# A routed mixture of experts behind attention: when a small block's weights are requested, and the order of the first two blocks

## The chip, the cores and the metric

The kernel runs on one core of a Trainium2 chip. The metric is the device time of one execution in microseconds, the median of the runs shown. TensorE does matrix products, VectorE and ScalarE elementwise work and the eviction of products, GpSimd the indirect DMAs (gather and scatter of rows by an index), SyncE issues the other DMAs.

## The reference

Three stages follow one another; each token is a row of 384 numbers.

```python
def reference(...):
    attn_out = _attn_ref(q, k, v, a_re, a_im)       # 4 x 8 heads, 768 steps, 48 wide: a recurrent state
    x = attn_out.transpose(0, 2, 1, 3).reshape(3072, 384)
    x = np.maximum(np.maximum(x @ w1, x @ w2), x @ w3) @ w_out    # first, dense layer
    ...
    # second layer, 8 experts: each row goes to the one expert with the largest logit
    logits = normed(x) @ normed(expert_emb).T / tau
    expert_idx = np.argmax(logits, axis=1)
    for e in range(8):
        mask = expert_idx == e
        h = np.maximum(x[mask] @ w1[e], 0.0)        # w1[e]: 384 x 1024
        out[mask] = gate_w[mask, None] * (h @ w2[e])  # w2[e]: 1024 x 384
```

## The kernel before, in words

The first part (to about 592 us of the trace) computes attention and the dense layer and writes its 3072 rows to memory. A first routing, over the rows that were done early, has by then chosen the rows of the first blocks. The second part, `phase2` (L1325), is the layer of experts, and the change lies there.

**Blocks and steps.** Rows of one expert are gathered into blocks of 128. `STEPS` (L56) lists what is done in order: steps 0 and 1 are single blocks (blocks 0 and 1, of the same expert), steps 2 to 6 and 8 to 13 are pairs of blocks that share an expert's weights (256 rows), and step 7 is one single block. In a pair, each product is made of three with operands split into a high and a low part (fp32r); single blocks use fp32 for the first product. An expert with only a few rows left (at most 32) is a **small block**, done by `small` (L1271), a generator in pieces that are placed into the steps that `WITH` (L58) names: 4, 6, 8, 10 and 12.

**What a step issues.** The loop of `phase2` goes through the steps; in step k it calls `gather` (L1173) for the rows of step k+2 on GpSimd, `load(k + 1)` (L1159) for the expert's weights, and `prep` (L1181), which copies and splits these weights into the form the products use (ScalarE copies to `w1s` and `w2h`, L1197 and L1206; VectorE subtracts to `w1l` and `w2l`, L1207). Then come the two halves of the first product, `mm1` (L1230: eviction to `hhi` on ScalarE, L1249, and to `hlo` on VectorE, L1250), `transpose` of the next step's gathered rows (L1217), and the second product `mm2` (L1254), which ends in a scatter of the rows to `out` on GpSimd. A small block of step k+1 begins in step k: its expert number is read on SyncE, both its weights are requested (`w1m`, L1281, and `w2m`, L1282), and its rows are gathered. Its products stand between the step's.

**What sets the order.** The program is written in the order above, and a scheduler moves instructions within each engine; afterwards each engine and each DMA queue works strictly in its own order. All weight DMAs go through SyncE. The regular weights have a ring of two slots (`QD = 2`): `load(k)` waits for a slot whose last reader (a copy or a subtraction in `prep`) is done. A load is conditional (`cond=c`): in this run's data six of the loads name the expert before and are skipped. `w1m` and `w2m` have one buffer each (`bufs=1`), so the DMA of the next small block waits until the small block before has made its first product (for `w1m`) or its second (for `w2m`). While SyncE waits there, everything behind it waits.

**The opening.** Steps 0 and 1 are run together (L1380 to L1383): step 0's products, then step 1's rows transposed, then step 1's first product. In these steps and the next two, `late_route` (L1066) runs on VectorE: the routing of the remaining rows, in two pieces (`LATE = 1, 1`, both placed behind step 1), whose end gives the list `src` from which the blocks of step 4 and later are gathered. The routing's tables lie in a pool (`rtp`) that is closed then, and the small blocks' weights (`mp`) take its place.

Of the kernel before, what the change touches and what calls it, by code (L numbers as in the profile page):

```python
# [9 lines left out]
F32 = mybir.dt.float32  # L10
# [15 lines left out]
DM = H * D  # L26
# [19 lines left out]
def steps(order):  # L46

    out, p, s = [(0, 1), (1, 1)], 2, KP
    for c in order:
        out.append((p, 2) if c == "p" else (s, 1))  # L50
        p, s = (p + 2, s) if c == "p" else (p, s + 1)
    assert (p, s) == (KP, NBLK - SPARE)
    return out + [(i, 1) for i in range(s, NBLK)]


STEPS = steps("ppppp" "s" "pppppp")  # L56

WITH = 4, 6, 8, 10, 12  # L58
NE, NS = 1 + PE, len(STEPS)

TESTS = 6 * NU + 6 + NTILE
# [252 lines left out]
class Prog:  # L314
# [956 lines left out]
    def small(self, pool, mp, pg, m):  # L1271


        nc = self.nc
        t, v, s, g = nc.tensor, nc.vector, nc.scalar, nc.gpsimd
        i, KD, KF, Q = NBLK + m, DM // 128, FF2 // 128, FF2 // 4
        e = nc.values_load(self.mtab[0:1, m:m + 1], engines=[ET.SP], min_val=0, max_val=E - 1,
                           skip_runtime_bounds_check_because="a count of 8 comparisons, of which one fails")
        w1 = mp.tile([128, KD, FF2], F32, tag="w1m", bufs=1, name=f"w1m{m}")
        w2 = mp.tile([128, KF, DM], F32, tag="w2m", bufs=1, name=f"w2m{m}")  # L1280
        nc.sync.dma_start(w1, self.io["w21"][bass.ds(e, 1)].rearrange("a p (k f) -> p (a k) f", f=FF2))  # L1281
        nc.sync.dma_start(w2, self.io["w22"][bass.ds(e, 1)].rearrange("a p (k f) -> p (a k) f", f=DM))  # L1282
        xg = pool.tile([128, DM], F32, tag="xg", bufs=4, name=f"xgm{m}")
        g.indirect_dma_start(out=xg, out_offset=None, in_=self.x1d,
                             in_offset=bass.IndirectOffsetOnAxis(ap=self.src[:, i:i + 1], axis=0),
                             bounds_check=NT - 1, oob_is_err=False)
        yield
        px = pg.tile([128, KD, MT], F32, tag="px", bufs=2, name=f"pxm{m}")
        for k in range(KD):
            t.transpose(px[:, k], xg[:MT, k * 128:(k + 1) * 128], self.ident[:MT, :MT])  # L1290
        x = pool.tile([128, KD, MT], F32, tag="xT", bufs=2, name=f"xm{m}")
        s.copy(x, px)
        yield
        ph = pg.tile([128, Q], F32, tag="ph", bufs=3, name=f"phm{m}")
        for k in range(KD):
            for j in range(4):
                t.matmul(ph[j * MT:(j + 1) * MT], x[:, k], w1[:, k, j * Q:(j + 1) * Q], start=k == 0, stop=k == KD - 1,
                         skip_group_check=True)
        h = mp.tile([128, Q], F32, tag="hm", bufs=1, name=f"hm{m}")
        s.activation(h, ph, AF.Relu)  # L1300
        yield
        pt = pg.tile([128, 2, 128], F32, tag="px", bufs=2, name=f"pt{m}")
        for c in range(2):
            t.transpose(pt[:, c], h[:, c * 128:(c + 1) * 128], self.ident)
        hT = mp.tile([128, 2, 128], F32, tag="hT", bufs=1, name=f"hT{m}")
        v.tensor_copy(hT, pt)
        yield
        py = pg.tile([128, DM], F32, tag="py", bufs=2, name=f"pym{m}")
        for c in range(2):
            for j in range(4):  # L1310
                r = slice(j * MT, (j + 1) * MT)
                t.matmul(py[r], hT[:, c, r], w2[:, 2 * j + c], start=c == 0, stop=c == 1, skip_group_check=True)
        part = pool.tile([128, DM], F32, tag="yo", bufs=3, name=f"part{m}")
        s.copy(part, py)
        yield
        ps = pg.tile([128, DM], F32, tag="py", bufs=2, name=f"psm{m}")
        t.matmul(ps, self.four, part, start=True, stop=True)
        y = pool.tile([128, DM], F32, tag="yo", bufs=3, name=f"ym{m}")
        s.activation(y, ps, AF.Copy, scale=self.gate_of[:, i:i + 1])
        g.indirect_dma_start(out=self.io["out"], in_=y, in_offset=None,  # L1320
                             out_offset=bass.IndirectOffsetOnAxis(ap=self.dst[:, i - KE:i - KE + 1], axis=0),
                             bounds_check=NT - 1, oob_is_err=False)
        yield

    def phase2(self):  # L1325
        tc, nc = self.tc, self.nc
        with ExitStack() as ctx:
            regs = tc.queue_regs(depth=QD, engines=[ET.SP, ET.Activation, ET.DVE], name="wr")

            pool = ctx.enter_context(tc.tile_pool(name="m2", bufs=1, reuse_waits="tile"))  # L1330
            qp = ctx.enter_context(tc.tile_pool(name="wq", bufs=1, reuse_waits="tile"))
            q1 = qp.queue([128, 3072], F32, regs=regs, name="q1", contiguous=True)
            q2 = qp.queue([128, 3072], F32, regs=regs, name="q2", contiguous=True)
            pg = ctx.enter_context(tc.tile_pool(name="pg2", bufs=2, space=PSUM, reuse_waits="tile"))
            wq = ctx.enter_context(tc.tile_pool(name="ws", bufs=1, reuse_waits="tile"))

            late_ctx = ctx.enter_context(ExitStack())
            rp = late_ctx.enter_context(tc.tile_pool(name="rtp", bufs=1, reuse_waits="tile"))
            load, gather, prep, share, transpose, mm1, mm2, st = self.moe2(pool, wq, pg, regs, q1, q2)
            late = self.late_route(rp, pg)  # L1340
            gather(*STEPS[1])
            load(0)
            first = prep(*STEPS[0])
            for _ in range(2):
                next(first)
            last = NS - SPARE
            few = iter(())
            for k, (i, n) in enumerate(STEPS[:last]):
                if k + 2 < last:
                    gather(*STEPS[k + 2])  # L1350
                p, after = iter(()), k + 1 < last
                if k == 0:

                    share(*STEPS[:2])
                    p = first
                elif after:
                    load(k + 1)
                    p = prep(*STEPS[k + 1])
                if k + 1 in WITH:

                    small = self.small(pool, mp, pg, WITH.index(k + 1))
                    next(small)
                next(p, 0)
                if k != 1:
                    mm1(i, n, 0)

                for _ in few:
                    pass
                if k in WITH:
                    few = small_now  # L1370
                    next(few)
                if k + 1 in WITH:
                    small_now = small
                next(p, 0)
                if k != 1:
                    mm1(i, n, 1)
                next(few, 0)
                next(p, 0)
                if after:
                    transpose(*STEPS[k + 1])  # L1380
                if k == 0:

                    for h in range(2):  # L1383
                        mm1(*STEPS[1], h)
                for b in range(n):
                    next(p, 0)
                    mm2(i, n, b)
                    next(few, 0)
                for _ in p:
                    pass  # L1390
                for _ in range(LATE.count(k)):
                    next(late)
                if k == LATE[-1]:
                    late_ctx.close()

                    self.four = self.mask
                    nc.gpsimd.memset(self.four, 0.0)
                    nc.vector.tensor_reduce(self.four[:, :MT], self.ident.rearrange("p (j r) -> p r j", r=MT), axis=AX.X,
                                            op=ALU.add)
                    mp = ctx.enter_context(tc.tile_pool(name="mp", bufs=1, reuse_waits="tile"))  # L1400
# [289 lines left out]
```

## Time and profile before

| | |
|---|---|
| median of 3 runs | 877.92 us (877.83 to 882.82) |
| the profiled execution | 880.89 us |
| its span, from the first instruction to the last | 879.1 us |
| mean granted TensorE clock, share of full speed | 0.972 |
| second part, first to last product | 592.35 to 871.79 |

All rows come from the one profiled execution; its 880.89 holds the span and 1.8 us around it. In a timeline row the first number is the start in us from the span's start, the second the duration; then engine, line of the kernel, operation, out<-in (the programs' names, buffer numbers left out), shape and count; in brackets the idle time of the engine ahead of it and what ended that. A row may stand for several instructions, back to back (x3). A row of the windows view begins with the window's start and end, each cut at the first product of a step (the six shown are steps 3, 5, 8, 9, 10 and 11), and gives its length, the busy time of each engine with its instructions, the mean granted clock of TensorE, and the DMA engines' share and rate.

### The profile page before, as it was taken

The page shows a single profiled execution, that of the slowest core. Times are in us where ns is not written, and L with a number is a line of the kernel's source. Part 1 is how long each engine was busy: PE and PEld are TensorE (multiplying, and loading weights), DVE is VectorE, ACT ScalarE, POOL GpSimd, SP SyncE. Part 2 cuts the span into 40 slices and gives each one's busy share as a digit, 9 for nine tenths or more (in the row PEclk, how much of TensorE's full clock was granted, in tenths as well). Part 3 has the DMA queues.
Part 4 walks back from the last instruction along what each step waited for, and adds up shares of the span by engine and source line. Part 5 has one row for each costly group of instructions (what it writes and reads, how often), then busy time and mean ns, then how long its engine had stood idle before and what let it go on. Part 6 is the DMA issues. An engine that isn't in the chain of part 4 may idle for free. (4 is left out here: it accounts for less than half of the span.)

```text
span 879.1 us, 17501 instructions
## 1 busy us (share of the span) xinstructions
PE 814.8 (93%) x6741; PEld 716.4 (81%) x6741; DVE 643.7 (73%) x1371; ACT 434.3 (49%) x918; POOL 132.7 (15%) x195
## 2 busy tenths in 40 slices
PE   0877899999999999999999999998968989999996
PEld 0655697979897888889797978888968989889986
DVE  5998898899888899898898854447984553545531
ACT  7897636435554536564546241117334563645521
POOL 5541100010100000000001000021123313222201
PEclk9889899999999999999999999998997999999999
DMA  8641162433625170707162341050036757475200
GB/s 316 250 115 30 35 138 82 109 122 69 160 45 147 32 187 18 175 17 174 43 149 83 72 88 32 19 191 26 29 152 223 303 215 285 164 298 216 96 20 23
DMA packets 38989, 108.67 MB, mean 124 GB/s; under 512 B 5460, under 2 KB 27011, under 8 KB 35824
## 3 DMA queue, kind: packets, MB, share of 16 engines
q1 hardware_dynamic: 30032, 77.15, 30.6%
q0 software_dynamic: 8320, 29.52, 10.1%
q8 instruction: 55, 0.90, 0.5%
q10 hardware_dynamic: 544, 0.79, 0.3%
q14 instruction: 38, 0.31, 0.1%
HBM read 97.92 MB, written 10.62 MB: 123 GB/s over the span
## 5 line engine op out<-in xcount | busy, mean ns | idle before, releaser
L299 PE MATMUL ph<-xhi,whi 128*128 128x256 f32 x648 | 117.1, 289 | 0.4 <-DVE slotgate L299 0.4
L299 PE MATMUL ph<-xlo,whi 128*128 128x256 f32 x648 | 112.8, 283 | 0.0
L299 PE MATMUL ph<-xhi,wlo 128*128 128x256 f32 x648 | 112.8, 283 | 0.0
L299 PEld LDWEIGHTS ph<-xhi,whi 128*128 128x128 f32 x648 | 93.5, 191 | 2.7 <-PE slots L299 0.5
L299 PEld LDWEIGHTS ph<-xlo,whi 128*128 128x128 f32 x648 | 93.2, 192 | 0.0
L299 PEld LDWEIGHTS ph<-xhi,wlo 128*128 128x128 f32 x648 | 93.1, 191 | 0.0
L1245 PE MATMUL ph<-xh,w1s 128*128 128x256 f32 x264 | 77.0, 292 | 1.2 <-DVE hlo L1250 1.2
L1261 PE MATMUL py<-w2h,hhi 128*128 128x384 f32 x200 | 71.2, 356 | 5.6 <-ACT hhi L1249 5.6
L1207 DVE TENSOR_TENSOR w2l<-queue_q_buf,w2h 128x768 fp32r<-128x768 f32 x52 | 47.9, 954 | 38.2 <-ACT w2h L1206 38.0
L1245 PE MATMUL ph<-xh,w1l 128*128 128x256 f32 x264 | 74.6, 283 | 0.0
L1245 PE MATMUL ph<-xl,w1s 128*128 128x256 f32 x264 | 74.6, 283 | 0.0
L1261 PE MATMUL py<-w2h,hlo 128*128 128x384 f32 x200 | 70.7, 355 | 3.5 <-DVE hlo L1250 3.3
L1250 DVE SCALAR_TENSOR_TENSOR hlo<-ph,hhi 128x512 fp32r<-128x512 f32 x50 | 34.3, 687 | 50.6 <-ACT hhi L1249 50.6
L299 PE MATMUL px<-wo,h 128*128 128x392 f32 x192 | 71.2, 502 | 0.0
L1261 PE MATMUL py<-w2l,hhi 128*128 128x384 f32 x200 | 69.7, 348 | 0.0
L299 DVE TENSOR_TENSOR h<-ph,h 128x512 f32<-128x512 f32 x72 | 49.5, 688 | 25.7 <-PE ph L299 23.6
L299 PEld LDWEIGHTS pa<-S 112*128 112x128 f32 x384 | 50.1, 196 | 8.9 <-ACT kt L299 4.7
L299 PE MATMUL pa<-S 112*128 112x128 f32 x384 | 53.2, 282 | 4.2 <-ACT kt L299 4.2
L299 PE MATMUL py<-at,v 128*64 128x128 f32 (+1 forms) x576 | 56.4, 276 | 0.4 <-DVE at L299 0.4
L1249 ACT ACTIVATE hhi<-ph 128x512 fp32r<-128x512 f32 x50 | 29.6, 597 | 50.9 <-PE ph L1245 50.7
L1245 PEld LDWEIGHTS ph<-xh,w1s 128*128 128x128 f32 x264 | 50.4, 191 | 4.6 <-issue 2.5
L299 PE MATMUL py<-S,Ts 112*64 112x128 f32 x480 | 51.5, 291 | 0.0
(405 smaller groups left out, 1846.4 us busy)
## 6 DMA issues: line engine op xcount, KB each, us to landing
queue_q_buf<-w SPq DMA_DIRECT2D x26, 1536.0 KB
S<-QK SPq DMA_DIRECT2D x46, 289.1 KB
QKr<-qk SPq DMA_DIRECT2D x11, 768.0 KB
X<-a SPq DMA_DIRECT2D x10, 768.0 KB
w1m<-w SPq DMA_DIRECT2D x5, 1536.0 KB
w2m<-w SPq DMA_DIRECT2D x5, 1536.0 KB
v<-v POOLq DMA_DIRECT2D x24, 288.0 KB
x1d<-x1s SPq DMA_DIRECT2D x20, 192.0 KB
```

Source lines behind the costliest of these rows:

```text
L299: getattr(getattr(self.nc, c[0]), c[1])(*c[2], **c[3])
L1207: v.tensor_sub(lo, bv[:, c], hi.bitcast(F32))
L1245: t.matmul(ph[:, f], a, b, start=o == 0, stop=o == len(ops) - 1)
L1249: s.activation(hi, ph, AF.Relu).ins,
L1250: v.scalar_tensor_tensor(lo, ph, 0.0, hi.bitcast(F32), op0=ALU.max, op1=ALU.subtract).ins]
L1261: t.matmul(py, a[:, f, r], c[:, k % 4], start=o == 0, stop=o == 3 * KF - 1)
```

## The change

Three edits. (1) In `small` the tile and the DMA of the second weights `w2m` move behind a new `yield`, so they are requested by a second call of the generator; `phase2` makes that call at the start of the step in which the small block is computed, behind `load(k + 1)`. The gather of the small block's rows stays in the first call. (2) `WITH` names the steps 5, 7, 9, 11 and 12 in place of 4, 6, 8, 10 and 12, so the first call of the first small block comes in step 4's place of the loop and the last one's products stay in step 12. (3) In step 0 the transposition of step 1's rows comes ahead of step 0's first product.

```diff
-WITH = 4, 6, 8, 10, 12
+WITH = 5, 7, 9, 11, 12
...
         w1 = mp.tile([128, KD, FF2], F32, tag="w1m", bufs=1, name=f"w1m{m}")
-        w2 = mp.tile([128, KF, DM], F32, tag="w2m", bufs=1, name=f"w2m{m}")
         nc.sync.dma_start(w1, self.io["w21"][bass.ds(e, 1)].rearrange("a p (k f) -> p (a k) f", f=FF2))
-        nc.sync.dma_start(w2, self.io["w22"][bass.ds(e, 1)].rearrange("a p (k f) -> p (a k) f", f=DM))
         xg = pool.tile([128, DM], F32, tag="xg", bufs=4, name=f"xgm{m}")
         g.indirect_dma_start(out=xg, out_offset=None, in_=self.x1d,
                              in_offset=bass.IndirectOffsetOnAxis(ap=self.src[:, i:i + 1], axis=0),
                              bounds_check=NT - 1, oob_is_err=False)
+        yield
+
+        w2 = mp.tile([128, KF, DM], F32, tag="w2m", bufs=1, name=f"w2m{m}")
+        nc.sync.dma_start(w2, self.io["w22"][bass.ds(e, 1)].rearrange("a p (k f) -> p (a k) f", f=DM))
         yield
...
                     load(k + 1)
                     p = prep(*STEPS[k + 1])
+                if k in WITH:
+                    next(small_now)
                 if k + 1 in WITH:
 
                     small = self.small(pool, mp, pg, WITH.index(k + 1))
                     next(small)
                 next(p, 0)
+                if k == 0:
+                    transpose(*STEPS[1])
                 if k != 1:
                     mm1(i, n, 0)
...
-                if after:
+                if after and k:
                     transpose(*STEPS[k + 1])
```

On SyncE, before, the second small block's weights (`w1m1`, `w2m1`) stand together ahead of a regular load (`queue..._q1_buf` and `_q2_buf`, two halves of one expert's weights; the rows at L1160 to L1169 read the expert's number and the condition):

```order
L1281 DMA w1m1_8145<-w21 128x3072
L1282 ISA
L1282 DMA w2m1_8146<-w22 128x3072
L1160 TENSOR_LOAD btab_95
L1164 TENSOR_LOAD btab_95
L1166 ISA
L1169 COMPARE_AND_BRANCH
L1170 ISA
L1170 DMA queue_6759_q1_buf<-w21 128x3072
L1171 ISA
L1171 DMA queue_6760_q2_buf<-w22 128x3072
```

The same place now (a second branch with the same two regular DMAs, for the other slot, is left out):

```order
L1280 DMA w1m1_8398<-w21 128x3072
L1160 TENSOR_LOAD btab_95
L1164 TENSOR_LOAD btab_95
L1166 ISA
L1169 COMPARE_AND_BRANCH
L1170 ISA
L1170 DMA queue_6759_q1_buf<-w21 128x3072
L1171 ISA
L1171 DMA queue_6760_q2_buf<-w22 128x3072
...
L1288 DMA w2m1_8652<-w22 128x3072
```

The regular load now follows the first weights at once, and the second weights stand behind it. The order on SyncE over the second part is now: loads 4 and 5, `w1m0`, load 6, `w2m0`, load 7, `w1m1`, load 8, `w2m1`, load 9, `w1m2`, load 10, `w2m2`, load 11, `w1m3`, load 12, `w2m3`, `w1m4`, load 13, `w2m4`; before it was `w1m0`, `w2m0`, load 6, `w1m1`, `w2m1`, load 7, load 8, `w1m2`, `w2m2`, load 9, load 10, `w1m3`, `w2m3`, load 11, load 12, `w1m4`, `w2m4`, load 13.

On TensorE, before, at the start of the second part (`ph0_0`, `ph0_1` the first product of block 0, `pxg1` the transposition of block 1's rows, `py0` the second product of block 0):

```order
L1245 MATMUL ph0_0_0_6846<-xT0_99,w1s0_0_6828 128x128 x12
L1245 MATMUL ph0_1_0_6865<-xT0_99,w1s0_1_6829 128x128 x4
L1169 UNCONDITIONAL_BRANCH
L1245 MATMUL ph0_1_0_6865<-xT0_99,w1s0_1_6829 128x128 x8
L1222 MATMUL pxg1_0_6885<-ident_61,xg1_6770 128x128 x3
L1261 MATMUL py0_0_6926<-w2h0_0_6830,hhi0_0_0_6859 128x384
```

And now, `ph1_0` and `ph1_1` being the first product of block 1:

```order
L1222 MATMUL pxg1_0_6847<-ident_61,xg1_6770 128x128 x3
L1245 MATMUL ph0_0_0_6852<-xT0_99,w1s0_0_6828 128x128 x12
L1245 MATMUL ph0_1_0_6871<-xT0_99,w1s0_1_6829 128x128 x3
L1169 UNCONDITIONAL_BRANCH
L1245 MATMUL ph0_1_0_6871<-xT0_99,w1s0_1_6829 128x128 x9
L1245 MATMUL ph1_0_0_6890<-xT1_6846,w1s0_0_6828 128x128 x12
L1245 MATMUL ph1_1_0_6907<-xT1_6846,w1s0_1_6829 128x128 x12
L1261 MATMUL py0_0_6926<-w2h0_0_6830,hhi0_0_0_6865 128x384
```

The transposition moved to the front, and with it the first product of block 1 moved ahead of block 0's second product.

## Rows read from the trace of the kernel before

**Rows 1.** The page's first part: busy time, share of the span, instructions of each engine.

```profile
PE 814.8 (93%) x6741; PEld 716.4 (81%) x6741; DVE 643.7 (73%) x1371; ACT 434.3 (49%) x918; POOL 132.7 (15%) x195
```

**Rows 2.** Windows: us, PE busy, PEld, DVE, ACT, POOL, PEclk, DMA share, GB/s.

```profile
636.66:669.46 32.80, 23.57 (x154) 21.91 (x154) 22.11 (x42) 10.06 (x14) 9.34 (x8) 0.84 0.51 192
...
690.89:714.02 23.13, 20.60 (x133) 19.18 (x129) 9.87 (x12) 9.65 (x15) 4.71 (x5) 0.93 0.82 316
...
746.10:769.85 23.75, 21.73 (x172) 19.14 (x171) 12.48 (x15) 15.81 (x23) 7.66 (x7) 1.00 0.46 172
769.85:792.70 22.85, 20.66 (x133) 19.28 (x129) 9.87 (x12) 9.61 (x14) 4.62 (x5) 0.93 0.83 313
792.70:814.13 21.43, 21.43 (x172) 19.08 (x171) 11.92 (x14) 11.76 (x19) 5.66 (x5) 1.00 0.52 192
814.13:832.50 18.37, 18.37 (x133) 18.10 (x129) 9.96 (x12) 9.77 (x15) 5.58 (x4) 1.00 0.34 115
```

**Rows 3.** TensorE's timeline in the second part, the long waits.

```profile
661.30 0.90 PE L1222 MATMUL pxg<-ident,xg 128*128 128x128 f32 x3 [6.85 <-DMA xg<-x1d,srcrow]
...
663.46 0.90 PE L1222 MATMUL pxg<-ident,xg 128*128 128x128 f32 x3 [0.61 <-DMA xg<-x1d,srcrow]
...
705.36 0.44 PE L1261 MATMUL py<-w2h,hhi 128*128 128x384 f32 x1 [2.18 <-ACT hhi L1249]
...
751.39 0.34 PE L1290 MATMUL pxm<-ident,xgm 32*128 32x32 f32 x3 [0.82 <-DMA xgm<-x1d,srcrow]
...
755.27 0.39 PE L1245 MATMUL ph<-xh,w1s 128*128 128x256 f32 x1 [1.20 <-DVE hlo L1250]
```

**Rows 4.** ScalarE's timeline in the second part.

```profile
601.98 0.46 ACT L1224 COPY xT<-pxg 128x384 f32<-128x384 f32 x1
...
703.34 1.47 ACT L1197 COPY w1s<-queue_q_buf 128x1536 f32 x1 [6.61 <-DMA queue_q_buf<-w]
...
719.13 1.49 ACT L1197 CAST w1s<-queue_q_buf 128x1536 fp32r x1
...
746.88 2.85 ACT L1197 CAST w1s<-queue_q_buf 128x1536 fp32r x2 [4.07 <-DMA queue_q_buf<-w]
...
782.19 1.47 ACT L1197 CAST w1s<-queue_q_buf 128x1536 fp32r x1 [6.50 <-DMA queue_q_buf<-w]
```

**Rows 5.** SyncE's timeline: DMA issues in the second part.

```profile
652.73 0.34 SPq L1282 DMA_DIRECT2D w2m<-w  x1
...
680.22 0.33 SPq L1281 DMA_DIRECT2D w1m<-w  x1
...
691.02 0.33 SPq L1282 DMA_DIRECT2D w2m<-w  x1
...
692.67 0.33 SPq L1170 DMA_DIRECT2D queue_q_buf<-w  x1
...
771.75 0.34 SPq L1170 DMA_DIRECT2D queue_q_buf<-w  x1
```

**Rows 6.** VectorE's timeline in the second part.

```profile
608.91 0.69 DVE L1250 SCALAR_TENSOR_TENSOR hlo<-ph,hhi 128x512 fp32r<-128x512 f32 x1 [2.65 <-ACT hhi L1249]
...
635.67 0.36 DVE L1130 SCALAR_TENSOR_TENSOR slot<-incl,slot 128x192 f32<-128x192 f32 x1 [0.65 <-DVE slot L1129]
...
639.64 0.69 DVE L1250 SCALAR_TENSOR_TENSOR hlo<-ph,hhi 128x512 fp32r<-128x512 f32 x1 [0.87 <-ACT hhi L1249]
...
647.50 1.95 DVE L1139 TENSOR_TENSOR ohpos<-pos,posblk 128x768 bf16<-128x768 f32 x2 [0.80 <-PE slots L920]
...
682.72 2.69 DVE L1207 TENSOR_TENSOR w2l<-queue_q_buf,w2h 128x768 fp32r<-128x768 f32 x3
```

**Rows 7.** GpSimd's timeline: the gathers of step 4's rows.

```profile
653.18 2.17 POOL L1176 DMA_INDIRECT xg<-x1d,srcrow  x1 [14.43 <-DVE dstrow L1147]
655.65 1.03 POOL L1176 DMA_INDIRECT xg<-x1d,srcrow  x1 [0.30 <-issue]
```

**Rows 8.** The chain that ended last: start us, us, what.

```profile
853.52 2.58 DMA out<-yo,dstrow
```

## The prediction

> **What bounds the kernel now.** I read the page's first part, then the steps of the second phase one by one, then what TensorE waited for in the steps that are too long, and last the queues behind those waits. TensorE is busy 93% of the span [rows 1], so only its gaps, and the slow stretches that go with them, can be won. In the second phase a step of two blocks without a small block takes 18.37 us and one with a small block 21.43, both 100% busy at clock 1.00, which is 2.4 GHz [rows 2]. Three steps are longer with the same work: step 5 (no small block) 23.13, step 9 (none) 22.85, step 8 (one) 23.75. In the first two the clock averages 0.93: TensorE sat 2.18 us, and the work after it ran in part at 1.2 GHz. Step 3 takes 32.80, at clock 0.84.
>
> In step 5 the wait names a ScalarE eviction [rows 3], but ScalarE itself sat 6.61 us in front of it until a weight load landed, 6.50 in step 9, and 4.07 before step 8 [rows 4]. SyncE's queue says why these loads are late [rows 5]: it holds the DMAs of step 4's small block in order, the first weights of the next small block at 680.22 (their one buffer is free when the first product is done, 10.76 us into the step), its second weights at 691.02, 0.13 after the step's end, because their one buffer is read until then. The regular load behind them goes at 692.67, 1.65 later. Its slot was free long before: its last reader ended at 685.41 (682.72 + 2.69, [rows 6]), so it lost 7.3 us to the queue. The same happens twice more, the last time at 771.75.
>
> In step 3 TensorE waits 6.85 us for the gathered rows of the next step [rows 3]. That gather starts at 653.18 on GpSimd, when VectorE has finished the routing, and takes 2.17 to issue (the one behind it 1.03) [rows 7]; a small block's weights, sent at 652.73 [rows 5] and in the call before it, share the DMA engines.
>
> **The change, part by part.** No instruction is added but a reordered branch; what changes is order.
>
> Second weights a step later. Behind the first weights SyncE now meets the next regular load, and the second weights stand behind that. Working in offsets from a step's start, for the regular load behind a first-weights DMA (steps 5 and 9): first weights at 10.8, load 1.65 later. From the first of three DMAs sent together to the landing of the second took 12.32 us (691.02 to 703.34, [rows 4, 5]). So the load has landed at 23.1. ScalarE copies it 5.11 into the next step (719.13 less 714.02, [rows 2, 4]), which is 21.43 + 5.11 = 26.5: it lands 3.4 us ahead of need. For the load behind second weights, these go at the next step's start, the load lands at 0.1 + 12.3 = 12.4 into it and is read 5 us into the step after, at 23 or later: 10 us ahead. In step 8, where the single block delays the small block's second product to some 6 us into the step, it lands near 19 and is read at 25. So the three waits go: 23.13 - 18.37 = 4.76, 22.85 - 18.37 = 4.48, and 23.75 - 21.43 = 2.32, together **11.56 us**. The last is 0.82 for a small block's gathered rows plus 1.20 behind a late split on VectorE [rows 3] and rounding. What would be late next is the copy at 3.4 us of cover; if that cover is gone in one of the two places, a stop of step 5's kind comes back, 4.7. Every DMA is still issued, five pairs of them, so the bytes are the same. GpSimd's gathers for small blocks move with their steps; the last one has half a step of cover, and I put it at nothing, with 0.82 as the worst, from the one seen.
>
> First small block a step later. Step 3 no longer sends both weights of a small block ahead of the gather; it still sends the first weights (their buffer lies where the routing's tables were, free only then), and step 5's first regular load follows. The small block's own TensorE time, 3.06 us (21.43 - 18.37), moves from step 4 to 5, 6 to 7, 8 to 9 and 10 to 11, and costs nothing either way.
>
> Second block's rows transposed first. TensorE runs the first products of blocks 0 and 1 one after the other instead of waiting for block 0's eviction. That by itself only makes TensorE wait longer in step 3. What counts is VectorE, which is nearly without a gap from there to the gather. Its gaps in that stretch that end on TensorE's work are 2.65, 0.87 and 0.80 us [rows 6], 4.32 in all, and all three lie behind products that now come some 4 us earlier. Against that stands the rows' copy on ScalarE (0.46, [rows 4]) now ahead of VectorE's split, and a branch brought forward into the chain, which costs about what its twin did, 0.65 [rows 6]. About 0.3 us of small routing work goes into a gap before. 4.32 - 0.46 - 0.65 + 0.3 = 3.5 us that the gather starts earlier. Bounds: 1.5 if only the first gap closes (2.65 - 0.46 - 0.65), 4.3 if the costs hide.
>
> Then the gather's own time. Before, TensorE has the rows at 661.30, 5.95 us after the issue ended (653.18 + 2.17). A lone indirect DMA landed 2.58 after its start at 853.52 [rows 8]; if the 1.03 of an issue like the second gather's [rows 7] is part of that, it landed 1.55 after its issue, and 5.95 - 1.55 = 4.4 is the most to be won. With one transfer beside it instead of two or three the gain is between 0 and 4.4. I take 1.1, near the lower end, since the regular load starts just as the gather does. Together **4.6 us** (bounds 1.5 and 8.7).
>
> The rows show that the second gather's product came 2.16 us behind the first (663.46 after 661.30, [rows 3]): the gathers move one after the other while weights flow. The Trainium skill's page "DMA: Bandwidth & Descriptors", section "Queues, rings and completion order", says that each DMA engine takes turns between the queues that have work. By that rule fewer transfers queued ahead help the gather nothing as long as one is flowing, the 1.1 is 0, and the time comes out 1.1 higher. No row before shows a gather beside just one transfer.
>
> **The sum.** 880.89 - 11.56 - 4.6 = 864.7 for an execution like the profiled one. The median of the runs is 877.92, 2.97 under that execution, so 861.8, say **862 us**.
>
> **Rivals.**
> 1. One wait comes back: a first-weights DMA holds SyncE in mid-step, the load behind it has 3.4 us of cover, and a slower transfer uses that up in one step. For it: the cover is the smallest I find. Against: step 7 of before copies a load without a wait under like traffic [rows 4]. 862 + 4.7 = 866.5.
> 2. The opening gains nothing: VectorE's gaps close, but something of the new order fills them, and TensorE waits for the gather as before. For it: two bounds in a row. Against: the 2.65 is a plain wait for a slow product. 862 + 4.6 = 866.5.
> 3. The change does not do what it says: the regular loads are held not by the second weights but by their own slot. For it: a slot must be read empty before it is filled. Against: in step 5 the last reader of the slot ended at 685.41, 7.3 us before the load went. Then only the opening counts: 877.92 - 4.6 = 873.3.
> 4. Slower: the weights flow at less than half the rate, because three DMAs are now sent within 3 us in every step. The five regular loads (of steps 7, 8, 9, 11 and 12) then each stop ScalarE as in step 5, 5 x 4.7 = 23.5 against 16.2 won: 877.9 + 7.3 = 885. It decides where a load takes over 12.3 + 3.4 = 15.7 us from the first of its three DMAs. Against: the 12.3 was measured with three at once.
>
> **How the numbers follow.** Forecast 0.62, rivals 0.13, 0.13, 0.07 and 0.05. One per cent of 877.92 is 8.8 us, about what a measurement of this kernel tells from no change: under 869.1 counts as faster. Forecast and rivals 1 and 2 fall there, 0.88; rival 3 is within 1%, 0.07; rival 4 is slower, 0.05. The range: 857 with the opening at its upper end (861.8 - 4.1 = 857.7, rounded down), 869 with one wait back and the opening at its lower end (861.8 + 4.7 + 3.1 = 869.6, cut to 869). That leaves out about 0.15.
>
> **What would show it.** Right: steps 5 and 9 at 21.4 us now, steps 4, 6 and 10 at 18.4, all at clock 1.00; ScalarE without a wait on a weight load after step 4; regular loads on SyncE within 2 us of a first-weights DMA; the gather's issue near 649.7, and its rows at TensorE near 656.7. Wrong: any 2 us gap of TensorE behind an eviction after step 4, or the gather's issue still after 652.

## The result, and the profile after

The changed kernel takes **867.12 us** (864.6 to 867.95, 4 runs) beside 877.88 for the kernel before (4 runs): ratio 0.9883, 95% interval 0.9846 to 0.9921. It is 10.8 us faster; forecast were 15.9 (862 us, range 857 to 869). Its profiled execution took 866.84, span 865.1. One of the four executions of run a below took 1972.35 us, and its median is that of the other three.

First the page's first part, then the windows of steps 3 to 10, cut at each step's first product as in [rows 2] and with the same columns:

```profile
PE 809.8 (94%) x6741; PEld 712.8 (82%) x6741; DVE 643.4 (74%) x1371; ACT 435.1 (50%) x918; POOL 125.9 (15%) x195
```

```profile
632.81:666.72 33.91, 24.78 (x154) 22.94 (x153) 23.66 (x45) 14.38 (x18) 9.34 (x8) 0.80 0.40 137
666.72:684.36 17.64, 17.64 (x127) 17.64 (x127) 10.07 (x13) 10.18 (x14) 5.51 (x4) 1.00 0.83 302
684.36:705.80 21.44, 21.44 (x172) 19.09 (x171) 11.97 (x14) 11.76 (x19) 5.09 (x5) 1.00 0.73 257
705.80:723.82 18.02, 18.02 (x130) 17.75 (x126) 9.03 (x10) 9.28 (x14) 3.80 (x3) 1.00 0.96 401
723.82:736.21 12.39, 12.39 (x108) 11.32 (x108) 6.20 (x9) 8.70 (x13) 5.09 (x5) 1.00 0.43 146
736.21:756.17 19.96, 19.96 (x148) 18.55 (x146) 10.79 (x14) 11.04 (x16) 6.07 (x5) 1.00 0.66 218
756.17:777.60 21.43, 21.43 (x172) 19.08 (x171) 11.93 (x14) 11.76 (x19) 5.10 (x5) 1.00 0.73 278
777.60:795.97 18.37, 18.37 (x133) 18.10 (x129) 9.87 (x12) 9.67 (x15) 5.14 (x5) 1.00 0.57 223
```

From step 4 to step 10 every step is now 100% busy at clock 1.00; the small block's 3.06 us have moved into steps 5, 7 and 9 (that of step 7 runs over into step 8: 12.39 against 10.95, and 19.96 against 18.37 for a step without one). Of these steps only step 3 (the first line) is not better: 33.91 against 32.80, clock 0.80.

SyncE's and ScalarE's timelines, the rows that answer to [rows 4, 5]:

```profile
695.13 0.34 SPq L1280 DMA_DIRECT2D w1m<-w  x1
697.20 0.34 SPq L1170 DMA_DIRECT2D queue_q_buf<-w  x1
...
705.93 0.33 SPq L1288 DMA_DIRECT2D w2m<-w  x1
707.56 0.34 SPq L1170 DMA_DIRECT2D queue_q_buf<-w  x1
```

```profile
710.91 1.47 ACT L1197 CAST w1s<-queue_q_buf 128x1536 fp32r x1
```

The regular load goes 2.07 us behind the first weights, and the copy that reads it, 5.1 us into step 6, has no bracket: ScalarE did not wait. No weight load after step 3 is waited for.

The opening, GpSimd's gather and TensorE's use of its rows ([rows 3, 7]):

```profile
649.33 2.16 POOL L1176 DMA_INDIRECT xg<-x1d,srcrow  x1 [14.42 <-DVE dstrow L1147]
```

```profile
658.30 0.90 PE L1222 MATMUL pxg<-ident,xg 128*128 128x128 f32 x3 [6.30 <-DMA xg<-x1d,srcrow]
...
660.89 0.90 PE L1222 MATMUL pxg<-ident,xg 128*128 128x128 f32 x3 [1.05 <-DMA xg<-x1d,srcrow]
```

The gather starts earlier (653.18 before), but from its start to the use it takes 8.97 us instead of 8.12. The two profiled executions differ by 14.0 in span: 0.43 from an earlier first product, 2.31 up to the start of step 4 (77.11 to 74.80 after the first product), 11.26 behind it. The medians differ by 10.8 only, and the experiments show which part of the 14.0 is not the change's.

### The profile page after: what moved, and what is told of

Its sections match the earlier page's. It is cut to its first block, busy times and chain, and to the rows that moved or that the text cites. A ratio compares the mean times of both kernels' runs of the same rounds, so it can differ in the third digit from the quotient of the medians.

```text
span 865.1 us, 17503 instructions
## 1 busy us (share of the span) xinstructions
PE 809.8 (94%) x6741; PEld 712.8 (82%) x6741; DVE 643.4 (74%) x1371; ACT 435.1 (50%) x918; POOL 125.9 (15%) x195
## 5 line engine op out<-in xcount | busy, mean ns | idle before, releaser
L1261 PE MATMUL py<-w2h,hlo 128*128 128x384 f32 x200 | 68.8, 345 | 3.2 <-DVE hlo L1250 3.2
L299 DVE TENSOR_TENSOR at<-pa,mask 128x512 f32<-128x512 f32 x48 | 33.1, 689 | 25.3 <-PE pa L299 25.0
```

The lines of the kernel that those rows point to most:

```text
L299: getattr(getattr(self.nc, c[0]), c[1])(*c[2], **c[3])
L1261: t.matmul(py, a[:, f, r], c[:, k % 4], start=o == 0, stop=o == 3 * KF - 1)
```

## The experiments

In the table, "issue" is the start of step 4's gather after the second part's first product, "use" the time from there to TensorE's use of the rows, "step 4" the start of that step after the first product, all from the profile; the ratio is to the kernel before in the same session (its own median is that of the session of its profile).

| run | median us | ratio (95%) | issue | use | step 4 |
|---|---|---|---|---|---|
| before, first profile | 877.88 | | 60.83 | 8.12 | 77.11 |
| before, second profile | 878.17 | | 58.03 | 8.11 | 73.71 |
| changed kernel | 867.12 | 0.9883 (0.9846 to 0.9921) | 57.41 | 8.97 | 74.80 |
| changed kernel again | 866.43 | 0.9885 (0.9857 to 0.9913) | 57.40 | 8.82 | 74.08 |
| a: without edit 3 | 868.95 | 0.9906 (0.9878 to 0.9935) | 59.63 | 8.58 | 75.64 |
| b: edit 3 alone | 875.06 | 0.9977 (0.9963 to 0.9992) | 57.42 | 7.93 | 73.81 |
| c: edits 2 and 3 | 874.23 | 0.9954 (0.9929 to 0.9979) | 57.42 | 8.05 | 73.52 |
| d: edits 1 and 3 | 866.82 | 0.9880 (0.9824 to 0.9936) | 57.42 | 8.18 | 73.37 |
| e: both held | 860.96 | 0.9806 (0.9778 to 0.9834) | 57.41 | 4.33 | 68.17 |
| f: load held | 859.75 | 0.9801 (0.9782 to 0.9820) | 57.28 | 4.95 | 67.99 |
| f again | 859.94 | 0.9808 (0.9781 to 0.9835) | 57.29 | 4.76 | 68.82 |
| h: before, held | 870.98 | 0.9936 (0.9902 to 0.9969) | 58.03 | 4.17 | 68.19 |
| i: first weights twice | 866.09 | 0.9887 (0.9850 to 0.9924) | 57.41 | 8.32 | 73.34 |

### a: the changed kernel without the third edit

```diff
-                if k == 0:
-                    transpose(*STEPS[1])
...
-                if after and k:
+                if after:
                     transpose(*STEPS[k + 1])
```

> The changed kernel with its third edit undone (the second block's rows are transposed where they were before); the weights and the steps of the small blocks as changed. Theory (the two edits on the small blocks take away the three waits, 11.55 us, and the third edit alone brings the gather forward): steps 5, 8 and 9 stay without a wait; the gather of block 6 is issued some 60.8 us after the second part's first product, as before (653.18 - 592.35), and not 57.4 as in the changed kernel (649.33 - 591.92); median near 869.5, some 2.5 over the changed kernel. Rival (the opening gains nothing from the third edit): median 867, gather's issue at 57.4 as well.

Measured 868.95, 1.8 above the changed kernel (by the ratios 2.0, with intervals that overlap), no load waited for after step 3, and the issue at 59.63. The waits go without the third edit, as the theory has it. The issue was expected at 60.8; the kernel before has the same opening, so that figure does not stand still (below).

### b: the third edit alone

```diff
+                if k == 0:
+                    transpose(*STEPS[1])
...
-                if after:
+                if after and k:
                     transpose(*STEPS[k + 1])
```

> The kernel before with the third edit alone. Theory: the gather of block 6 is issued 57.4 us after the second part's first product instead of 60.8; the weights of the first small block still come ahead of it; the waits of steps 5, 8 and 9 stay (11.5 us); median 874.5 to 876, from 877.9. Rival (the third edit gains nothing): 877.9. A second rival (the waits go by the earlier opening, not by the order of the weights): steps 5, 8 and 9 at 18.4, 21.4 and 18.4, median under 870.

Measured 875.06, 1.7 under the kernel before in its session, with the stops of steps 5, 8 and 9 as before (TensorE 2.03, 1.20 and 1.92) and the issue at 57.42. The third edit alone is worth 1.7 us in the median; on top of the others it gave about as much (run a), though there the intervals overlap.

### c and d: which of the first two edits takes the waits away

c, the second weights requested with the first, the small blocks in the new steps; d, the second weights later, the small blocks in the old steps:

```diff
# c, against the changed kernel, in small()
+        w2 = mp.tile([128, KF, DM], F32, tag="w2m", bufs=1, name=f"w2m{m}")
         nc.sync.dma_start(w1, ...)
+        nc.sync.dma_start(w2, ...)
...
-        yield
-
-        w2 = mp.tile([128, KF, DM], F32, tag="w2m", bufs=1, name=f"w2m{m}")
-        nc.sync.dma_start(w2, ...)
         yield
# and in phase2()
-                if k in WITH:
-                    next(small_now)
```

```diff
# d, against the changed kernel
-WITH = 5, 7, 9, 11, 12
+WITH = 4, 6, 8, 10, 12
```

> The second and third edits without the first: small blocks in steps 5, 7, 9, 11 and 12, but both weights of a small block requested together, as before. Theory (a load that stands behind second weights, which wait for the end of a step, is late): the second weights of the second small block go at the start of step 6 and load 8 behind them 1.7 us later, while ScalarE reads it 5.1 us into step 6 in the changed kernel (710.91 - 705.80); it lands 12.3 after the first of three, so ScalarE waits some 7 us in step 6, and likewise in step 10, each a step of 23 us instead of 18.4; the stops have moved one step on and not gone. Median 874 to 877. Rival (moving the small blocks by a step is what takes the waits away): no wait over 1 us in steps 4 to 12, median 866 to 868.

> The first and third edits without the second: second weights a step later, the small blocks in their old steps 4, 6, 8, 10 and 12. Theory (the place of the second weights is what counts): regular loads go behind first weights some 12.4 us into steps 4 and 8, and land before ScalarE wants them 5 us into the next step; no wait of TensorE over 1.5 us after step 3; the opening as in the run with the third edit alone, since first and second weights of the first small block then both flow beside the gather; median 866 to 868.5. Rival (the shift by a step is needed): stops of TensorE as before in steps 5, 8 or 9, median 871 to 876.

c took 874.23. SyncE's, ScalarE's and TensorE's timelines of c show the stops moved on by a step:

```profile
706.74 0.33 SPq L1282 DMA_DIRECT2D w2m<-w  x1
708.81 0.34 SPq L1170 DMA_DIRECT2D queue_q_buf<-w  x1
```

```profile
718.63 1.47 ACT L1197 CAST w1s<-queue_q_buf 128x1536 fp32r x1 [5.93 <-DMA queue_q_buf<-w]
...
796.84 1.47 ACT L1197 CAST w1s<-queue_q_buf 128x1536 fp32r x1 [6.01 <-DMA queue_q_buf<-w]
```

```profile
720.65 0.44 PE L1261 MATMUL py<-w2h,hhi 128*128 128x384 f32 x1 [2.10 <-ACT hhi L1249]
...
798.86 0.44 PE L1261 MATMUL py<-w2h,hhi 128*128 128x384 f32 x1 [1.58 <-ACT hhi L1249]
```

The second weights go at the start of step 6 (706.61), the load 2.1 behind, it lands 12.0 into the step, and ScalarE had wanted it at 6.1. Steps 6 and 10 take 24.47 and 22.43 us at clock 0.86 and 0.92, where the changed kernel has 18.02 and 18.37 at 1.00. d took 866.82, the same as all three edits, and ScalarE waits for no load there; its longest wait of TensorE after step 3 is 0.43, for a small block's gathered rows. Windows of d, its steps 5, 8 and 9:

```profile
687.35:705.71 18.36, 18.36 (x133) 18.09 (x129) 9.87 (x12) 9.65 (x15) 4.06 (x4) 1.00 0.84 340
737.80:759.71 21.91, 21.48 (x172) 19.09 (x171) 11.97 (x14) 12.02 (x19) 8.64 (x8) 1.00 0.56 188
759.71:778.08 18.37, 18.37 (x133) 18.11 (x130) 9.87 (x12) 9.62 (x14) 4.06 (x4) 1.00 0.82 328
```

So the first edit, beside the third, takes the stops of steps 5 and 9 away, and the second adds nothing on top that these runs can tell. The third stop, step 8's, is gone in c too, where ScalarE waits for two loads and not three: either edit takes that one away.

### e and f: nothing beside the gather

Both are the changed kernel. In e a DMA of one element from block 7's gathered rows into the first weights' buffer stands ahead of the weights' own DMA; in f it goes to a spare tile ahead of load 6. SyncE waits at it until the rows have landed. In the cuts of e, f and h the two lines that keep block 7's tile are left out.

```diff
# e, in small()
+        if m == 0:
+            nc.sync.dma_start(w1[:1, 0, :1], self.rows[:1, :1])    # self.rows: xg of block 7
         nc.sync.dma_start(w1, ...)
# f, in phase2()
+                    if k == 5:
+                        nc.sync.dma_start(pool.tile([1, 1], F32, tag="hold", name="hold"), st["rows"][:1, :1])
                     load(k + 1)
```

> The changed kernel, with the first small block's first weights held, and the regular load behind them on SyncE's queue with them, until the gathered rows of block 7 have landed (a DMA of one element from those rows into the weights' buffer stands ahead of the weights). Theory (the gather is slowed by weights that flow beside it): from the issue's start to TensorE's use of block 6's rows 4 to 5.5 us instead of 8.97 (658.30 - 649.33), median 862.5 to 864. Rival (the gather needs that long by itself, whatever flows beside it): 8.5 to 9 us, median 867 or above. Both: no new wait behind, since the held weights are first read 25 us later.

> The changed kernel, with only the regular load behind the first small block's first weights held until block 7's rows have landed (a DMA of one element from those rows to a spare tile stands ahead of it); the first weights flow ahead of the gather as in the changed kernel. Theory (each transfer that is flowing slows the gather): from the issue's start to TensorE's use of block 6's rows 4.5 to 6.5 us, median 863 to 865, a little over the run that holds both. Rival (the gather needs that long by itself): 8.5 to 9 us, median 867. Rival (the first weights, ahead of the gather, are what slows it): as in the changed kernel, 867.

e took 860.96 and f 859.75: both beat the changed kernel and the one before. e is 1.5 us under the least that was expected and f 3.2, and f is not over e as it should have been. GpSimd's and TensorE's rows of e:

```profile
649.70 2.17 POOL L1176 DMA_INDIRECT xg<-x1d,srcrow  x1 [14.42 <-DVE dstrow L1147]
```

```profile
654.03 0.55 PE L1224 MATMUL pxg<-ident,xg 128*128 128x128 f32 x3 [1.48 <-DMA xg<-x1d,srcrow]
```

The use comes 4.33 us after the issue instead of 8.97, and TensorE waits 1.48 instead of 6.30. It is the weights that flow beside the gather that slow it. In e the held load is late once, against the expectation: ScalarE waits 1.62 us for it in step 4, and TensorE has no wait over 0.3 us behind that. In f the first weights still go ahead, and it is 4.95: they cost 0.6, the load behind them the other 4. Windows of f and then of the changed kernel, from 650 to the use, say why the two differ so:

```profile
650.00:652.00 2.00, 2.00 (x8) 2.00 (x8) 2.00 (x5) 0.01 (x1) 2.00 (x1) 0.50 0.99 418
652.00:654.79 2.79, 0.59 (x2) 0.08 (x2) 1.64 (x5) 1.55 (x2) 2.04 (x3) 0.88 0.58 175
```

```profile
650.00:652.00 2.00, 1.99 (x7) 1.48 (x5) 2.00 (x5) 0.61 (x1) 1.70 (x2) 0.50 0.94 369
652.00:653.00 1.00, 0.00 (x0) 0.00 (x0) 1.00 (x4) 0.95 (x2) 0.82 (x1) 0.86 0.51 172
653.00:658.30 5.30, 0.00 (x1) 0.01 (x1) 0.12 (x2) 0.00 (x0) 2.01 (x2) 0.75 0.94 337
```

In both the rate (the last column, GB/s) falls at 652, to 175 and 172, when, as far as the rates tell, the first weights are through. In f it stays low until the use; in the changed kernel load 6, sent at 650.70, brings it to 337. In e step 4 then starts some 6.6 us earlier (74.80 to 68.17): 4.64 from the use, the rest from TensorE's stretch behind it. Windows of the changed kernel and of f again, from issue to use and from use to step 4:

```profile
649.33:658.30 8.97, 2.67 (x10) 2.16 (x9) 3.79 (x8) 1.56 (x2) 5.20 (x4) 0.69 0.90 329
658.30:666.72 8.42, 7.37 (x27) 6.86 (x27) 4.93 (x7) 1.54 (x3) 3.16 (x3) 0.55 0.34 102
```

```profile
649.92:654.68 4.76, 2.13 (x9) 1.61 (x7) 3.78 (x8) 1.56 (x2) 4.15 (x3) 0.51 0.74 265
654.68:661.45 6.77, 6.77 (x26) 6.67 (x27) 4.59 (x7) 1.54 (x3) 3.19 (x4) 0.59 0.68 200
```

The clock is low behind the wait in both (0.55 and 0.59), but in f again TensorE no longer waits for the second block's rows, which is 1.05 of the 1.65 us between 8.42 and 6.77.

### h: the same hold in the kernel before

```diff
+        if m == 0:
+            nc.sync.dma_start(w1[:1, 0, :1], self.rows[:1, :1])
         nc.sync.dma_start(w1, ...)
         nc.sync.dma_start(w2, ...)
```

> The kernel before, with both weights of the first small block and the load behind them held until the rows of block 7 have landed (a DMA of one element from those rows into the weights' buffer ahead of them). Theory (transfers beside the gather cost the opening some 4 us and its low clock another 2, in the kernel before as in the changed one): from the gather's issue to its use 4.3 to 5 us instead of 8.12, step 3 some 5 us shorter, the stops of steps 5, 8 and 9 unchanged; median 870 to 872. Rival (the held weights are then late for step 4, where the small block reads them 8 us into the step): the gain is given back in step 4, median 875 or above.

Measured 870.98, use 4.17 after the issue. The gather's delay was there before, as large; ScalarE's waits stay (5.20, 3.86, 6.49), and the held weights are late for nobody.

### A second profile of the kernel before

> The kernel before, unchanged, for a second profile. Theory (the stops behind loads last as long in every profiled execution, and the profiled execution of this kernel is some 3 us over its median): ScalarE waits 6.0 to 7.0 us for the loads in steps 5 and 9, TensorE 2 us, and the gather takes 7.5 to 8.5 from issue to use; profiled time 878 to 882. Rival (the stops vary from one execution to the next): one of them differs by over 1 us from the first profile.

The profiled time is 877.87, 3.0 under the first profile and on the median. ScalarE's waits for loads (6.55, 3.72 and 6.40) and the use (8.11) are within 0.4 of the first's; the rival, that something varies by over 1 us, is right in the opening alone. Windows of steps 0 and 1, first profile, with the two microseconds in it at half clock, and then the second profile:

```profile
592.35:618.90 26.55, 23.92 (x158) 23.32 (x157) 20.99 (x51) 19.27 (x32) 2.57 (x3) 0.87 0.11 31
602.00:604.00 2.00, 2.00 (x9) 2.00 (x8) 2.00 (x3) 2.00 (x5) 0.00 (x0) 0.50 0.00 0
```

```profile
592.91:616.66 23.75, 21.12 (x158) 20.46 (x157) 20.92 (x51) 19.26 (x32) 2.58 (x3) 1.00 0.12 35
```

In the first profile TensorE fell to 1.2 GHz about 601, at the second of two gaps of 1.35 and 1.28 us (it was busy 1.37 of the 4 us from 598 to 602), and steps 0 and 1 took 2.80 us longer. In the second it had the same two gaps at the same place (busy 1.38 of these 4 us) and stayed at 2.4 GHz. VectorE's gap of 2.65 [rows 6] is not there at all. Run a is in between (clock 0.93, gap 1.44, issue 59.63); h is like the second profile. With the third edit all nine profiles have clock 1.00 in steps 0 and 1 and an issue of 57.28 to 57.42: one gap of 0.95 is left there. In the four profiles with the old opening (60.83, 58.03, 59.63 and 58.03) the issue is on average 1.7 us later than 57.4, as much as run b won in the median. So the third edit's worth seems to lie mostly in the dip that no longer comes; four profiles are too few to show it.

### i: the first weights requested twice

```diff
         nc.sync.dma_start(w1, ...)
+        if m:
+            nc.sync.dma_start(w1, ...)
```

> The changed kernel with the first weights of each small block but the first requested twice, one DMA behind the other into the same buffer (a suspected cost doubled; nothing is left out). It measures the cover of the regular loads that stand behind first weights (loads 8 and 12), which the prediction put at 3.4 us. The load comes later by the second DMA: by some 3.9 us if SyncE sends it at once (1.5 MB at the 400 GB/s of the windows), by 5 to 7 if it waits for the first to land. Theory (cover 3.4): ScalarE waits 0.5 us for load 8 in step 6 and load 12 in step 10 in the first case, 2 to 4 in the second, and TensorE stops by at most 1.5 in each; median 867 to 870. Rival (cover under 1, so that the change stands close to a new stop): ScalarE waits 3.5 to 7, median 870 to 875. Rival (cover over 7): no wait of ScalarE on a load, median 867.

SyncE sent the second DMA 7.6 us after the first, so it waited, as the expectation's second case has it, for the first to land (the landing itself is not in these rows):

```profile
692.25 0.34 SPq L1280 DMA_DIRECT2D w1m<-w  x1
...
699.84 0.33 SPq L1282 DMA_DIRECT2D w1m<-w  x1
701.90 0.34 SPq L1170 DMA_DIRECT2D queue_q_buf<-w  x1
```

```profile
711.07 1.48 ACT L1197 CAST w1s<-queue_q_buf 128x1536 fp32r x1 [2.94 <-DMA queue_q_buf<-w]
...
782.63 1.47 ACT L1197 CAST w1s<-queue_q_buf 128x1536 fp32r x1 [2.52 <-DMA queue_q_buf<-w]
```

Load 8 goes 20.42 us into step 5 (which starts at 681.48), 7.58 later than in the changed kernel (697.20 - 684.36 = 12.84), and ScalarE waits 2.94 for it: a cover (the time from a load's landing to its reading) of 4.6 (3.4 forecast). Load 12 gives 4.3 in the same way (6.77 later, 2.52 waited). TensorE has no wait of 0.3 us there, and the median is 866.09: behind ScalarE's cover lies another 2.9 at least.

### The changed kernel and f once more

> The best version so far once more, beside the changed kernel on the same chip: the regular load behind the first small block's first weights held until block 7's rows have landed. Theory: 859 to 861, 6 to 8 us under the changed kernel in the same session; from the gather's issue to its use 4.5 to 5.5 us. Rival (the gain was one session's): within 3 us of the changed kernel.

> The changed kernel once more, for a second profile and a second median. Theory (no load is waited for after step 3, and the opening no longer has the gaps behind which TensorE's clock fell in the first profile of the kernel before): no wait of TensorE over 0.5 us after step 3; clock 1.00 in steps 0 and 1; the gather's issue 57.4 us after the first product; from there to its use 7.9 to 9 us; median 865 to 868. Rival (the opening varies as before): clock under 0.95 in steps 0 and 1, issue later than 58.

Measured 859.94 and 866.43 in one session: holding load 6 is worth 6.5 us on top of the change. The changed kernel's second profile has no wait over 0.5 after step 3, clock 1.00 in steps 0 and 1, the issue at 57.40 and the use 8.82 later.

## Why the prediction was right and where it was not

**The waits: right.** 11.56 were forecast to go. Behind the start of step 4 the span shrank by 11.26 against the first profile and by 11.00 against the second (209.38 to 198.38). Steps 5 and 9 are at 21.4 and steps 4, 6 and 10 at 17.6 to 18.4, all at clock 1.00, as said. That the order on SyncE's queue held the loads, and not their slots, is shown by c and d: with the second weights back in front, the stops of steps 5 and 9 are back, a step later. The step 8 term (2.32) came out as well: steps 7 and 8 together went from 34.70 to 32.35.

**The cover: right in kind, small by a quarter.** 3.4 us were found, 4.3 to 4.6 measured (run i): the load goes 12.84 into the step (12.4 forecast), in run i it lands 9.2 after it is sent (711.07 - 701.90), which would be at 22.0 here, and it is read at 26.55. Rivals 1 and 4 needed that cover to go and did not come about; rival 3 fell with c and d.

**VectorE's 3.5 us in the opening: wrong in size.** The step that failed is "4.32 - 0.46 - 0.65 + 0.3 = 3.5 us that the gather starts earlier". It is 3.42 against the first profile and 0.62 against the second (58.03 to 57.41). The gap of 2.65 on which it stood was a product at 1.2 GHz in that one execution, and the forecast read it as "a plain wait for a slow product" that every execution has. Without it the same sum gives 0.87 + 0.80 - 0.46 - 0.65 + 0.3 = 0.86, near the 0.62.

**The median: counted twice.** "The median of the runs is 877.92, 2.97 under that execution, so 861.8" took the excess of the profiled execution for something that stays. As far as the two profiles of the kernel before show, it was the 2.80 us of the same slow stretch (26.55 against 23.75), which the sum had just removed through VectorE's gap. The changed kernel's profiled execution stands 0.3 under its median, not 3.0 above. This and the 3.5 are one error seen from two sides: from the first profile the 3.5 was right and nothing was left to subtract, from the second the subtraction was right and the 3.5 was 0.62. It is 2.9 of the 5.3 us between 861.8 and 867.12, about half. Not every excess over a median lies there: the profiled executions of b and c stand 4.1 and 3.9 over theirs, with clock 1.00 in steps 0 and 1.

**The gather's own time: wrong in sign.** "the gain is between 0 and 4.4. I take 1.1" came out as -0.86 against the second profile (8.11 to 8.97), and the second block's rows came later too (a wait of 1.05 instead of 0.41), so that from use to step 4 it is 8.42 instead of 7.57 there. That is 2.8 us less than forecast, the other half (the waits fell 0.56 short, and the first product came 0.99 earlier). Against that profile the opening is then 1.09 us longer (73.71 to 74.80: 0.62 won, 0.86 and 0.85 lost), and the whole is 11.00 - 1.09 and 0.99 from an earlier first product, which scatters from 590.5 to 594.0 over these profiles: 10.9, the difference of the spans (876.0 to 865.1). The forecast had counted how many transfers stand beside the gather; e and f show that a single one, load 6, costs 4 us, and that none may flow beside the rows: f's first weights were all but through by then. The bound of 4.4 us for a gather left alone was good: h, the kernel before with the hold, won 8.11 - 4.17 = 3.9.

The sentence on the Trainium skill, page "DMA: Bandwidth & Descriptors", section "Queues, rings and completion order" (an engine takes turns between the queues with work), pointed the right way, and the traces agree: with load 6 still flowing beside it (337 GB/s) the gather gained nothing (8.97 against 8.12), and in f, where the rate falls to 175, it gained 4.0.

**Rival 2 in effect.** Against the second profile the opening as a whole gained nothing, as the rival with a chance of 0.13 had it (866.5 us), though by another way: VectorE's gaps did close and the gather is issued at 649.33 (forecast 649.7), but its rows are used at 658.30 and not at 656.7. That 867.12 lies within 857 to 869 is in part luck: the upper end was made for a wait that comes back (4.7) and an opening that gains 1.5, no wait came back, and its room took up an opening below that bound.

What stays open is why the gather is slower by some 0.5 us with edits 1 and 2 together (8.32 to 8.97 in a, i and both profiles of the changed kernel) than without one of them (7.93 to 8.18 in b, c, d and before). In the four slower ones one DMA of weights stands ahead of load 6 and not two, and less flows from issue to use (329 to 347 GB/s against 416 to 428); no run takes this apart.

## What to carry to other kernels

In a queue that is worked in order, place a DMA whose buffer comes free late behind those that could go at once: one edit of this kind took all the stops away here, and moving the work itself by a step instead moved two of the three and took one away. A small gather on which an engine waits is best left alone on the DMA engines: holding one bulk load, which the changed kernel reads 15.6 us after it uses the rows (673.89 - 658.30), until they had landed was worth 6.5 us beside the change's 10.8. Before an excess of the profiled execution over the median is subtracted from a forecast, find where in the trace it lies, with a second profile: here it lay, as far as two profiles tell, in the very gap that the change closes.

## What the runs showed that was not expected

TensorE's clock behind short gaps is not the same from one execution to the next: with the same two gaps of 1.35 and 1.28 us it stayed at 1.00 in two profiles (the second of before, and h), and averaged 0.93 and 0.87 over steps 0 and 1 in two others (a, and the first of before), which took 1.6 and 2.8 us more there. With one gap of 0.95 it stayed at 1.00 in all nine. A gather of 128 rows takes 4.2 to 5.0 us from its issue to its use where load 6 is held back, and 7.9 to 9.0 beside bulk loads, with 329 to 428 GB/s on the DMA engines in that time.
